# Gated recurrence and a squared-ReLU MLP on one core: a block's last w_out products behind the next block's first w_in products, and keys and queries one piece earlier

## The chip, the cores and the metric

One core of one Trainium2 chip. The metric is the device time of one execution in microseconds (us), compared as the median of several runs of each kernel on the same chip. The kernel before takes 506.82 us (median of 3 runs, 506.09 to 507.06).

## The reference

Two stages, the second on the first one's output:

```python
f = 1.0 / (1.0 + np.exp(-f_logit))              # batch 4, 8 heads, 768 steps, width 48
for t in range(S):
    state = f[:, :, t, :, None] * state + np.einsum('bhd,bhe->bhde', k[:, :, t], v[:, :, t])
    y[:, :, t] = np.einsum('bhd,bhde->bhe', q[:, :, t], state)
x = y.transpose(0, 2, 1, 3).reshape(3072, 384)
h = x @ w_in                                    # 384 x 2048
g = np.maximum(h, 0.0) ** 2
out = g @ w_out                                 # 2048 x 384
```

## The kernel before

**Blocks and units.** The 768 steps are six blocks of 128; with the batch of 4, a block is 512 columns of x. A block's recurrence is computed in four units (pairs of heads; the fourth is put together from leftover rows of the other three). `Unit` has stages that are named by letters: L and v load, G is the sigmoid of the gates (ScalarE, L426), K the keys (a scan and a product on VectorE, L431 and L437, with two clamps on GpSimd, L436), Q the queries (reciprocal, scan, product: L443, L445, L448), T and N transpose the keys (TensorE L481, ScalarE copies), D and S are products on TensorE (L505, L516), M and C mask and carry the state on VectorE (L523, L538, L543), Y the outputs on TensorE (L564, L576), H and X split the result into the two float32r parts of x (ScalarE L593, VectorE L598). After a fourth unit, `parts` (L605) moves the leftover rows from the tile `ys` into x by six small DMAs.

**The MLP.** `Moe` walks over 16 slices f of the hidden width. A piece n is `up(f)`: nine matmuls of 128x512 with w_in into a PSUM bank `ph` (L247), then ScalarE's ReLU, square and cast to `gh` (L257 to L259) and VectorE's `rest`, the remainder `gl` (L264), which frees the bank; and, two pieces later (LAG = 2), `down(f)`: nine matmuls with w_out into the three banks `po` (L273). There are two banks `ph` in turn, so `up(f)` waits until `rest(f-2)` is done; only the last block has a third bank. `run` writes this order out:

```python
for n in range(len(self.fs) + LAG):
    if n < len(self.fs):
        ...            # up, square, rest of slice n, with hooks between
    if n >= LAG:
        self.down(self.fs[n - LAG])
    for hook in hooks.get((n, 1), ()):
        hook()
```

So a block ends with two `down` in a row, and the next one begins with three `up` in a row, since it has no `down` of its own before its third piece. Between them `finish` (L317) copies the three `po` to SBUF (`ob`, ScalarE and VectorE) and issues three DMAs to the output on SyncE's queue (L326); for the second half of block 0 it adds them on VectorE to `part`, what `keep` saved of the first half (L310), and sends `part` out (L322, L326).

**Order of the work.** All four engines' orders are as written: the table FIRST and SECOND for block 0's and block 1's units and the first eight slices of block 0, then the list `order`: block 1, the second half of block 0 (slices 8 to 15), blocks 2, 3, 4, 5. This document calls the six places between them B1 (first half of block 0 to block 1), B2 (block 1 to second half of block 0), B3 (to block 2), B4 (2 to 3), B5 (3 to 4) and B6 (4 to 5). `up`, `down`, `rest` with a prime, as `up(0')`, are the block's that begins there. The 16 later units (blocks 2 to 5) are hooked to pieces, counted through all blocks: SLOTS gives each unit's piece `at` (D, S, M, C there, Y of the unit before it), and STAGE_AT puts the other stages some pieces ahead, at a place in the piece (0 before `up`, 0.5 before `rest`, 0.7 behind it, 1 behind `down`). Unit slot 18 is the third piece after B2.

**Shared buffers.** `ob`, `gh` and `gl` share tags of three buffers each. `part` shares one buffer with `junk`, into which ScalarE writes while `sizes` (L157) sums the weights, one product per piece in blocks 2 and 3; the first of these hooks is at piece 0 of block 2, so it waits until `part` has gone out.

Of the kernel before, what the change touches and what calls it, by code (L numbers as in the profile page):

```python
# [12 lines left out]
F32 = mybir.dt.float32  # L13
# [7 lines left out]
ALU = mybir.AluOpType  # L21
ET = mybir.EngineType

P = 128
# [7 lines left out]
NT = B * TB  # L32
# [3 lines left out]
NJ = DM // P  # L36
# [9 lines left out]
LAG = 2  # L46
# [10 lines left out]

STAGE_AT = ((-5, 0, "Lv"), (-2, 1, "GK"), (-1, 0.5, "Q"), (-1, 1, "TN"))  # L60
LAST_AT = ((-5, 0, "v"),)

SLOTS = (12, 14, 18, 20, 22, 28, 31, 34, 37, 44, 47, 50, 53, 60, 63, 66, 69)
# [11 lines left out]
c3 E0 W0 A4 i5 o2 R1 A7 O1 h3 d1 U2 C4 s4 o3 I4 B2 J3 M4 Y4 E1 U3 i6 Q5 c4 P1 W1 R2 E2 H4 X4 L6 G6 K6 o4  # L75
R3 J4 O2 v5 B3 S5 A5 U4 I5 M5 c5 d2 O3 E3 d3 D5 P2 C5 I7 r5 T6 J5 N6 P3 s5 A6 B4 I6 c6 o6 W2 O4 Q6 Y5 H5
X5 o5 U5 B5 W3 B7 B6 c7 R4 J6 m5 O6 R5 J7 E4 D6 S6 v7 C6 m6 r6 s6 U7 M6 O5 d5 Y6 d6 E5 d4 H6 X6 U6 P5 O7
P4 D7 S7 C7 r7 M7 R6 E6 P6 W4 s7 Y7 H7 X7 R7 h7 E7 W5 g7 d7 P7 W6 W7
"""


class Moe:
# [182 lines left out]
            out=gl, in0=self.ph.pop(f), in1=gh.bitcast(F32), op=ALU.subtract  # L265
        )

    def down(self, f, es=range(NJ)):
        gh, gl = self.g[f]
        for e in es:  # L270
            wh, wl = (self.w[f, 1][:, i, e * P : (e + 1) * P] for i in range(2))
            for i, (l, r) in enumerate(((wh, gl), (wl, gh), (wh, gh))):
                self.nc.tensor.matmul(  # L273
                    self.po[e], lhsT=l, rhs=r, start=f == self.fs[0] and i == 0,
                    stop=f == self.fs[-1] and i == 2,
                )

    def run(self, hooks, obs=None):

        for n in range(len(self.fs) + LAG):  # L280
            self.at = n
            if obs and n == len(self.fs):
                for e in range(NJ):
                    for f in self.fs[-LAG:]:
                        self.down(f, (e,))
                    for _, cs in tails(e):
                        self.nc.vector.tensor_copy(out=obs[e][:, cs], in_=self.po[e][:, cs])
                return
            if n < len(self.fs):
                for hook in hooks.get((n, 0), ()):  # L290
                    hook()
                f = self.fs[n]
                self.up(f)
                self.square(f)
                for hook in hooks.get((n, 0.5), ()):
                    hook()
                self.rest(f)
                for hook in hooks.get((n, 0.7), ()):
                    hook()
            if n >= LAG:  # L300
                self.down(self.fs[n - LAG])
            for hook in hooks.get((n, 1), ()):
                hook()
# [3 lines left out]
        t = self.gp.tile([P, NJ, NZ * CZ], F32, tag="part", name=name, bufs=1)  # L307
        return [t[:, e, :NT] for e in range(NJ)]

    def keep(self):  # L310

        part = self.third_of(f"part{self.blk}")
        for e in range(NJ):
            (self.nc.vector.tensor_copy if e % 2 else self.nc.scalar.copy)(out=part[e], in_=self.po[e])
        return part

    def finish(self, dst, part=None):  # L317
        nc = self.nc
        for e in range(NJ):
            if part:  # L320
                ob = part[e]
                nc.vector.tensor_tensor(out=ob, in0=self.po[e], in1=ob, op=ALU.add)  # L322
            else:
                ob = self.gp.tile([P, NT], F32, tag=("gh", "gl")[e % 2], name=f"ob{self.blk}_{e}")
                (nc.vector.tensor_copy if e % 2 else nc.scalar.copy)(out=ob, in_=self.po[e])
            nc.sync.dma_start(dst(e), ob)  # L326


def tails(e):

    if e < NJ - 1:
        return ((1, slice(0, NT)),)
    return ((0, slice(0, NT // 2)), (1, slice(NT // 2, NT)))
# [10 lines left out]
def fast_path(ctx, tc, moe, ident, low, fkqT, vN, w, w4, out):  # L344
    nc = tc.nc
# [20 lines left out]
    for r in (0, C):  # L366
        G.affine_select(
            out=mask[r : r + C], in_=mask[r : r + C], compare_op=ALU.is_ge, fill=0.0,
# [12 lines left out]
    def weights_load(f, i, mark=False):  # L381
        raw = moe.words(f, i)
        if mark:

            V.memset(raw[0:1, 0:1], 0)
        nc.sync.dma_start(raw, w[f, i].bitcast(I16)[:, 1:])
# [254 lines left out]
    xs = {blk: moe.new_x(blk, blk) for blk in range(2)}  # L641
# [66 lines left out]
    with tc.manual_schedule(engines={ET.PE, ET.SP, ET.DVE, ET.Activation}):  # L708
        with tc.tile_pool(name="ps_p", bufs=2, space=bass.MemoryType.PSUM) as ps_p:
            for t in FIRST.split():  # L710
                step(t)
        moe.psum(ctx, "ps_h1", "ps_o")

        moe.sums_of()
        for t in SECOND.split():
            step(t)
        part = moe.keep()
        whole = half[0] + half[1]
        order = [(1, whole), (0, half[1])] + [(blk, whole) for blk in range(2, NBLK)]
        hooks = [{} for _ in order]  # L720

        def hook(k, n, at, do):
            while n >= len(order[k][1]):
                k, n = k + 1, n - len(order[k][1])
            hooks[k].setdefault((max(n, 0), at), []).append(do)

        def third():
            early.close()
            moe.inputs(ctx)
            xs[2] = moe.new_x(2, 2)  # L730

        halves = [(f, i) for f in half[1] for i in range(2)]
        steps = {}

        def advance(h):
            if h not in steps:
                steps[h] = moe.decode(moe.row[halves[h]], lambda: moe.parts(*halves[h]))
            next(steps[h], None)  # L740

        for n in range(1, NF - 1):
            few = range(3 * (n - 1) // 2, min(3 * n // 2, len(halves)))
            for h in few:
                if n < AHEAD:
                    weights_load(*halves[h])
                else:
                    hook(0, n - AHEAD, 0.5, lambda h=h: weights_load(*halves[h], mark=True))

            def before(few=few):  # L750
                for h, last in zip(few, (None, *few)):
                    for m in (h, h, last):
                        if m is not None:
                            advance(m)

            def after(few=few[:-1]):
                for h in few:
                    advance(h)

            def last(few=few):  # L760
                for h in few[-1:]:
                    advance(h)
                    advance(h)


            for place, do in zip((0, 0.5, 0.7) if n > 1 else (0.7, 0.7, 0.7), (before, after, last)):
                hook(0, n, place, do)
        hook(0, 12, 0, third)
        later = [Unit(n, xs, (ps_a,)) for n in range(2 * HP, NBLK * HP)]
        for un, last, at in zip((*later, None), (None, *later), SLOTS):  # L770
            if un:
                for n, place, stage in STAGE_AT if un.own else LAST_AT:
                    hook(0, at + n, place, lambda un=un, stage=stage: un.stage(stage))

            def slot(un=un, last=last):
                for who, stage in (last, "Y"), (un, "DS"), (last, "HX"), (un, "rMC"), (un, "m" * bool(un and un.own)):
                    if who:
                        who.stage(stage)
                if last and not last.own:
                    last.stage("hg")  # L780

            hook(0, at, 0.7, slot)
            if un:
                hook(0, at + 1, 0, lambda un=un: un.stage("s"))

        for n in range(2 * NF):
            hook(2 + n // NF, n % NF, 1, lambda n=n: moe.sizes(n // 2, n % 2))
        general = []
        found = verdict(nc, moe, low, ident, ps_a)
        for n in range(2):  # L790
            hook(len(order) - 2, VERDICT_AT + n, 1, lambda: general.append(next(found)))
        hook(
            len(order) - 1, VERDICT_AT, 1,
            lambda: general.append(nc.values_load(general[1][0:1, 0:1], min_val=0, max_val=1)),
        )
        for k, (blk, fs) in enumerate(order):
            if blk > 1 and blk + 1 < NBLK:
                xs[blk + 1] = moe.new_x(blk + 1, (0, 1, 2)[blk - 2])
            moe.start(blk, xs[blk], fs)
            if blk == NBLK - 1:  # L800

                moe.third_bank = ps_a
                obs = moe.third_of("ob_last")
                moe.run(hooks[k], obs)
                moe.third_bank = None
            else:
                moe.run(hooks[k])
                moe.finish(lambda e: out[blk, e * P : (e + 1) * P], None if blk else part)
    return general[2], obs


# [203 lines left out]
```

## Time and profile before

| | |
|---|---|
| median of 3 runs | 506.82 us (506.09 to 507.06) |
| profiled execution | 504.94 us, of which span 503.2 us |
| PE (matmul) busy | 481.3 us, 96% of the span |
| ACT busy | 294.1 us, 58% |
| DVE busy | 237.8 us, 47% |
| POOL busy | 28.4 us, 6% |
| mean granted TensorE clock | 0.996 |

PE is TensorE's matmul, PEld its weight load, DVE VectorE, ACT ScalarE, POOL GpSimd, SP SyncE, whose queue (SPq) issues most DMAs. "idle before <-releaser" is the time an engine stood still before an instruction and what ended it. The chain of waits follows the work that ended last back to the start. Matmuls overlap in the records, so a nine of 128x512 products is read from where one nine starts to where the next does.

### The profile page before, as it was taken

The numbers are of one execution on the slowest core, as the hardware profiler recorded it, in microseconds if no ns is written. First come the engines' busy times: TensorE is split into PE (matmuls) and PEld (weight loads), VectorE is DVE, ScalarE is ACT, GpSimd is POOL, SyncE is SP. The second block draws the span as 40 slices with busy tenths as digits, with TensorE's granted clock in tenths as the row PEclk, the third lists the DMA queues.
The fourth block names the chain that finished last, engine by engine and source line by source line (L and its number), as shares of the span: only waits on it lengthen the run. The fifth ranks groups of instructions, "written<-read, shape, count | busy, mean of one in ns | idle before, by whom it ended". The sixth has DMA issues, their size and how long they took to land.

```text
span 503.2 us, 11462 instructions
## 1 busy us (share of the span) xinstructions
PE 481.3 (96%) x4831; PEld 383.7 (76%) x4831; DVE 237.8 (47%) x444; ACT 294.1 (58%) x615; POOL 28.4 (6%) x66
## 2 busy tenths in 40 slices
PE   3979999999998999999999999999999999999995
PEld 2667777888786887788888788888788877888884
DVE  7979963556734472563361444352346232211112
ACT  5569875877545553766664767564565544544441
POOL 6131010000000000000000000000000000000000
PEclk9999999999998999999999999999999999999999
DMA  8978007560214017203014313004410002100001
GB/s 263 310 259 278 13 7 245 187 228 27 89 29 151 3 18 196 62 17 90 3 26 136 102 28 92 1 7 117 141 29 12 1 1 33 64 1 1 0 1 68
DMA packets 20588, 41.96 MB, mean 83 GB/s; under 512 B 2752, under 2 KB 6192, under 8 KB 20528
## 3 DMA queue, kind: packets, MB, share of 16 engines
q1 hardware_dynamic: 19936, 40.09, 25.8%
q0 software_dynamic: 448, 0.92, 0.9%
q8 instruction: 40, 0.66, 0.6%
q14 instruction: 20, 0.16, 0.1%
q10 hardware_dynamic: 144, 0.13, 0.1%
HBM read 31.68 MB, written 4.72 MB: 72 GB/s over the span
## 4 chain that ended last, share of the span: by engine, by line
PE 90%; DVE 3%; ACT 3%; DMA 1%; issue 1%; SPq 0%; POOL 0%; ACTq 0%
PE po L273 41%; PE ph L247 38%; PE ds L516 2%; PE ds L505 2%; PE py L564 2%; PE pk L481 2%; PE ph L564 1%; PE ph L576 1%; DVE fkq L431 1%; PE py L576 1%; DMA vn<-in_vN_dram 1%; PE ph L667 1%; ACT gh L259 1%; ACT ph L257 1%; ACT ph L258 1%
## 5 line engine op out<-in xcount | busy, mean ns | idle before, releaser
L247 PE MATMUL ph<-x,w 128*128 128x512 f32 x864 | 219.8, 400 | 4.8 <-DVE sc L523 2.7
L247 PEld LDWEIGHTS ph<-x,w 128*128 128x128 f32 x864 | 161.6, 189 | 44.6 <-POOL low L436 3.0
L273 PE MATMUL po<-gh,w 128*128 128x512 f32 x576 | 180.9, 395 | 0.0
L264 DVE TENSOR_TENSOR gl<-ph,gh 128x512 fp32r<-128x512 f32 x96 | 66.3, 690 | 225.1 <-ACT gh L259 225.0
L257 ACT ACTIVATE ph<-ph 128x512 f32<-128x512 f32 x96 | 56.0, 583 | 129.5 <-PE ph L247 129.5
L273 PEld LDWEIGHTS po<-gh,w 128*128 128x128 f32 x576 | 108.3, 188 | 25.1
L273 PE MATMUL po<-gl,w 128*128 128x512 f32 x288 | 115.9, 403 | 0.6 <-DVE gl L264 0.6
L273 PEld LDWEIGHTS po<-gl,w 128*128 128x128 f32 x288 | 54.1, 188 | 14.5 <-DVE gl L264 1.3
L259 ACT CAST gh<-ph 128x512 fp32r<-128x512 f32 x96 | 56.3, 587 | 3.0
L258 ACT ACTIVATE ph<-ph 128x512 f32<-128x512 f32 x96 | 55.9, 582 | 3.0
L436 POOL TENSOR_SCALAR fkq<-fkq 128x8 f32<-128x8 f32 x18 | 11.0, 609 | 307.0 <-DVE fkq L431 263.9
L475 ACT COPY sx<-sp 48x208 f32<-48x208 f32 x44 | 16.0, 365 | 15.5 <-DVE sp L538 15.2
L431 DVE TENSOR_TENSOR_SCAN fkq<-fz,dr 128x520 f32<-128x520 f32 x18 | 22.2, 1232 | 1.1 <-ACT fz L426 1.1
L445 DVE TENSOR_TENSOR_SCAN fkq<-fz,dz 128x520 f32<-128x520 f32 x18 | 22.4, 1242 | 0.6
L131 ACT CAST head<-raw 128x384 f16<-128x384 bf16 (+1 forms) x33 | 19.3, 627 | 4.9 <-DMA raw<-in_w_dram 4.8
L564 PEld LDWEIGHTS py<-sc,vn 64*48 64x48 f32 (+1 forms) x384 | 16.2, 126 | 7.3 <-issue 7.3
L564 PE MATMUL py<-sc,vn 64*48 64x64 f32 (+1 forms) x384 | 20.6, 222 | 0.0
L576 PE MATMUL py<-rx,sx 48*48 48x64 f32 x192 | 19.3, 215 | 0.0
L143 ACT CAST w<-wa 128x384 fp32r<-128x384 f32 (+1 forms) x33 | 16.5, 510 | 3.6 <-DVE wa L134 3.2
L145 DVE TENSOR_TENSOR w<-wa,w 128x384 fp32r<-128x384 f32 (+1 forms) x33 | 17.9, 548 | 1.1 <-ACT w L143 0.6
L481 PE MATMUL pk<-ident,fkq 128*128 128x128 f32 x72 | 12.0, 293 | 6.3 <-POOL x L700 3.9
L134 DVE SCALAR_TENSOR_TENSOR wa<-raw,head 128x384 int32<-128x384 int32 (+1 forms) x33 | 17.6, 548 | 0.7 <-ACT head L131 0.6
(104 smaller groups left out, 462.6 us busy)
## 6 DMA issues: line engine op xcount, KB each, us to landing
raw<-in_w_dram SPq DMA_DIRECT2D x32, 383.8 KB, 5.8
fkq<-in_fkqT_dram SPq DMA_DIRECT2D x15, 768.0 KB, 5.0
vn<-in_vN_dram SPq DMA_DIRECT2D x24, 192.0 KB, 4.8
out_dram<-ob SPq DMA_DIRECT2D x12, 256.0 KB, 2.1
fkq<-in_fkqT_dram SPq DMA_DIRECT2D x9, 256.0 KB, 6.1
x<-ys SPq DMA_DIRECT2D x30, 64.0 KB, 2.4
last_kq<-fkq SPq DMA_DIRECT2D x28, 64.5 KB, 2.3
out_dram<-part SPq DMA_DIRECT2D x3, 256.0 KB, 2.1
```

What stands on the lines that cost most here:

```text
L131: nc.scalar.copy(out=self.upper(head, F16), in_=high)
L247: self.nc.tensor.matmul(self.ph[f], lhsT=w[:, i], rhs=x[:, j], start=first and n == 0, stop=last and n == 2)
L257: nc.scalar.activation(ph, ph, AF.Relu)
L258: nc.scalar.activation(ph, ph, AF.Square)
L259: nc.scalar.copy(out=gh, in_=ph)
L264: self.nc.vector.tensor_tensor(out=gl, in0=self.ph.pop(f), in1=gh.bitcast(F32), op=ALU.subtract)
L273: self.nc.tensor.matmul(self.po[e], lhsT=l, rhs=r, start=f == self.fs[0] and i == 0, stop=f == self.fs[-1] and i == 2,)
L431: V.tensor_tensor_scan(out=rr[:, ::-1], data0=self.fz[:, NZ * CZ : 0 : -1], data1=dr[:, ::-1], initial=0.0, op0=ALU.mult, op1=ALU.add,)
L445: V.tensor_tensor_scan(out=pp, data0=self.fz[:, : NZ * CZ], data1=dz, initial=0.0, op0=ALU.mult, op1=ALU.add)
L481: nc.tensor.transpose(out=self.pk[:, b], in_=self.kt[:, b * TB : (b + 1) * TB], identity=ident)
L564: nc.tensor.matmul(self.py[c][h * C : h * C + m, b * C : (b + 1) * C], lhsT=self.vn[rows, b, h * D : h * D + m], rhs=self.sc[rows, h, b], ...
L576: nc.tensor.matmul(self.py[c][h * C : h * C + m, b * C : (b + 1) * C], lhsT=s[rows, b * D : b * D + m], rhs=q[rows], start=False, stop=b = ...
```

## The change

It has two parts. First, `down` of a block's last slice no longer stands at the end of that block: `run` stops before it, and the next block's `run` calls it (with the evacuation of `po` behind it) after its own first `up`, square and `rest`. The last block still ends as before. Second, STAGE_AT puts G and K of the later units at the end of piece at-3 (it was at-2) and Q into piece at-2 (it was at-1); loads, T and everything from the slot on stay.

```diff
-STAGE_AT = ((-5, 0, "Lv"), (-2, 1, "GK"), (-1, 0.5, "Q"), (-1, 1, "TN"))
+STAGE_AT = ((-5, 0, "Lv"), (-3, 1, "GK"), (-2, 0.5, "Q"), (-1, 1, "TN"))
...
-P4 D7 S7 C7 r7 M7 R6 E6 P6 W4 s7 Y7 H7 X7 R7 h7 E7 W5 g7 d7 P7 W6 W7
+P4 D7 S7 C7 r7 M7 R6 E6 P6 W4 s7 Y7 H7 X7 R7 h7 E7 W5 g7 d7 P7 W6
...
-    def down(self, f, es=range(NJ)):
-        gh, gl = self.g[f]
+    def down(self, f, es=range(NJ), of=None):
+        po, g, fs = of or (self.po, self.g, self.fs)
+        gh, gl = g[f]
...
-    def run(self, hooks, obs=None):
+    def run(self, hooks, obs=None, before=None):
+
 
         for n in range(len(self.fs) + LAG):
+            if before and not obs and n == len(self.fs) + LAG - 1:
+                return
...
+            if before and n == 0:
+                before()
+                self.sums_of()
             if n >= LAG:
                 self.down(self.fs[n - LAG])
...
+    def ending(self, end):
+
+        of, f = (self.po, self.g, self.fs), self.fs[-1]
+
+        def do():
+            self.down(f, of=of)
+            end(of[0])
+
+        return do
...
-        part = moe.keep()
+        part = []
+        owed = moe.ending(lambda po: part.extend(moe.keep(po)))
...
-            moe.start(blk, xs[blk], fs)
+            moe.begin(blk, xs[blk], fs)
...
-                moe.run(hooks[k], obs)
+                moe.run(hooks[k], obs, owed)
...
-                moe.run(hooks[k])
-                moe.finish(lambda e: out[blk, e * P : (e + 1) * P], None if blk else part)
+                moe.run(hooks[k], None, owed)
+                owed = moe.ending(
+                    lambda po, blk=blk: moe.finish(
+                        lambda e: out[blk, e * P : (e + 1) * P], None if blk else part, po, blk
+                    )
+                )
```

**PE at B3.** `po_8_*` is the second half of block 0, `ph_0`, `ph_1` and `ph_2` are block 2's first slices. PE before, at the end of the second half of block 0:

```order
L273 MATMUL po_8_0_1987<-gl_15_2452,w_1_1682 128x512
L273 MATMUL po_8_0_1987<-gh_15_2451,w_1_1682 128x512 x2
L273 MATMUL po_8_1_1988<-gl_15_2452,w_1_1682 128x512
L273 MATMUL po_8_1_1988<-gh_15_2451,w_1_1682 128x512 x2
L273 MATMUL po_8_2_1989<-gl_15_2452,w_1_1682 128x512
L273 MATMUL po_8_2_1989<-gh_15_2451,w_1_1682 128x512 x2
L247 MATMUL ph_0_2496<-x_0_1706,w_0_375 128x512 x3
L247 MATMUL ph_0_2496<-x_1_1707,w_0_375 128x512 x3
L247 MATMUL ph_0_2496<-x_2_1708,w_0_375 128x512 x3
L247 MATMUL ph_1_2514<-x_0_1706,w_0_360 128x512 x3
```

PE now, at the same place:

```order
L247 MATMUL ph_0_2478<-x_0_1711,w_0_375 128x512 x3
L247 MATMUL ph_0_2478<-x_1_1712,w_0_375 128x512 x3
L247 MATMUL ph_0_2478<-x_2_1713,w_0_375 128x512 x3
L274 MATMUL po_8_0_2011<-gl_15_2452,w_1_1682 128x512
L274 MATMUL po_8_0_2011<-gh_15_2451,w_1_1682 128x512 x2
L274 MATMUL po_8_1_2012<-gl_15_2452,w_1_1682 128x512
L274 MATMUL po_8_1_2012<-gh_15_2451,w_1_1682 128x512 x2
L274 MATMUL po_8_2_2013<-gl_15_2452,w_1_1682 128x512
L274 MATMUL po_8_2_2013<-gh_15_2451,w_1_1682 128x512 x2
L247 MATMUL ph_1_2514<-x_0_1711,w_0_360 128x512 x3
```

The old block's last nine stands between the new block's first and second nine; behind it `up(1')`, `up(2')` and `down(0')` follow as before. B1, B2, B4, B5 and B6 change in the same way.

**DVE at B2.** `gl_15` is block 1's last remainder, `gl_8` and `gl_9` the first two of block 0's second half; the `fkq_2` rows (a scan, shown as SCALAR_TENSOR_TENSOR, a product, a reciprocal, a scan, a product) are K and Q of the unit at slot 18. DVE before, at block 1's end:

```order
L264 TENSOR_TENSOR gl_15_1946<-ph_15_1842,gh_15_1945 128x512
L325 COPY ob_1_1981<-po_0_1_1262 128x512
L264 TENSOR_TENSOR gl_8_2001<-ph_8_1990,gh_8_2000 128x512
L431 SCALAR_TENSOR_TENSOR fkq_2_1785<-fz_71,dr 128x520
L437 TENSOR_TENSOR fkq_2_1785<-fkq_2_1785 128x512
L443 RECIPROCAL dz<-fkq_2_1785 128x8
```

DVE now, at the same place:

```order
L264 TENSOR_TENSOR gl_15_1946<-ph_15_1842,gh_15_1945 128x512
L448 SCALAR_TENSOR_TENSOR fkq_2_1788<-fz_71,dr 128x520
L454 TENSOR_TENSOR fkq_2_1788<-fkq_2_1788 128x512
L460 RECIPROCAL dz<-fkq_2_1788 128x8
L462 SCALAR_TENSOR_TENSOR fkq_2_1788<-fz_71,dz 128x520
L465 TENSOR_TENSOR fkq_2_1788<-fkq_2_1788 128x512
L264 TENSOR_TENSOR gl_8_1985<-ph_8_1974,gh_8_1984 128x512
L342 COPY ob_1_2005<-po_0_1_1284 128x512
L264 TENSOR_TENSOR gl_9_2029<-ph_9_2018,gh_9_2028 128x512
```

Keys and queries moved ahead of the new block's first remainder, and the copy of `po` behind it.

**DVE and ACT at B3.** `gl_0` to `gl_2` are block 2's first remainders. DVE before, at the end of the second half of block 0:

```order
L264 TENSOR_TENSOR gl_15_2452<-ph_15_2339,gh_15_2451 128x512
L322 TENSOR_TENSOR part_1249<-po_8_0_1987,part_1249 128x512
L322 TENSOR_TENSOR part_1249<-po_8_1_1988,part_1249 128x512
L322 TENSOR_TENSOR part_1249<-po_8_2_1989,part_1249 128x512
L264 TENSOR_TENSOR gl_0_2507<-ph_0_2496,gh_0_2506 128x512
L264 TENSOR_TENSOR gl_1_2525<-ph_1_2514,gh_1_2524 128x512
L264 TENSOR_TENSOR gl_2_2546<-ph_2_2535,gh_2_2545 128x512
L431 SCALAR_TENSOR_TENSOR fkq_1_2438<-fz_71,dr 128x520
```

DVE now, at B3:

```order
L264 TENSOR_TENSOR gl_0_2489<-ph_0_2478,gh_0_2488 128x512
L339 TENSOR_TENSOR part_1279<-po_8_0_2011,part_1279 128x512
L339 TENSOR_TENSOR part_1279<-po_8_1_2012,part_1279 128x512
L339 TENSOR_TENSOR part_1279<-po_8_2_2013,part_1279 128x512
L264 TENSOR_TENSOR gl_1_2525<-ph_1_2514,gh_1_2524 128x512
L448 SCALAR_TENSOR_TENSOR fkq_1_2438<-fz_71,dr 128x520
```

ACT now, at B3, with the semaphores that each instruction waits for (DMAHW is a DMA's; the three here are those of the DMAs that send `part` out):

```order
L259 CAST gh_0_2488<-ph_0_2478 128x512 [waits Activation_49]
L157 ACTIVATE junk,sums<-w_0_375 128x384 [waits DMAHW4_49,DMAHW5_49,DMAHW3_49,DVE_49]
L257 ACTIVATE ph_1_2514<-ph_1_2514 128x512 [waits PE_49]
L258 ACTIVATE ph_1_2514<-ph_1_2514 128x512 [waits Activation_49]
L259 CAST gh_1_2524<-ph_1_2514 128x512 [waits Activation_49]
```

The three additions to `part` moved behind `gl_0`, and K (with Q behind it) ahead of `gl_2`. On ACT these five rows stand in the same order, with the same waits, as before.

## Rows read from the trace of the kernel before

**Rows 1.** The page, part 1: busy us (share of the span) xinstructions of TensorE.

```profile
PE 481.3 (96%) x4831; PEld 383.7 (76%) x4831; DVE 237.8 (47%) x444; ACT 294.1 (58%) x615; POOL 28.4 (6%) x66
```

**Rows 2.** Waits of PE, longest first: us in total, times, longest us.

```profile
PE pk L481 <- DVE fkq L437: 2.4, 1, 2.4
PE ph L247 <- DVE gl L264: 1.6, 3, 0.5
PE ph L247 <- DVE raw L385: 0.5, 1, 0.5
```

**Rows 3.** The chain of waits at B4 and B6: start us, us, what.

```profile
275.23 2.12 PE ph L247 x9
279.96 2.38 PE ph L247 x9
282.34 2.10 PE po L273 x9
...
430.64 6.32 PE ph L247 x27
```

**Rows 4.** The chain: a piece with T undisturbed, and B2's first and third nine.

```profile
123.90 2.10 PE po L273 x9
126.43 2.11 PE ph L247 x9
...
151.38 2.12 PE ph L247 x9
...
159.12 3.01 PE ph L247 x9
```

**Rows 5.** Stretches at B2: busy us (xinstructions) of each engine, PEclk, DMA share, GB/s.

```profile
155.60:158.00 2.40, 0.00 (x1) 0.00 (x1) 2.31 (x3) 1.93 (x4) 0.64 (x1) 0.91 0.67 250
158.00:161.00 3.00, 3.00 (x9) 2.57 (x10) 2.74 (x4) 0.70 (x2) 0.27 (x2) 0.50 0.00 0
```

**Rows 6.** DVE's timeline, keys and queries in block 2: start us, us, instruction [idle before].

```profile
221.20 0.69 DVE L264 TENSOR_TENSOR gl<-ph,gh 128x512 fp32r<-128x512 f32 x1 [3.04 <-ACT gh L259]
221.81 1.23 DVE L431 TENSOR_TENSOR_SCAN fkq<-fz,dr 128x520 f32<-128x520 f32 x1
...
226.02 0.68 DVE L264 TENSOR_TENSOR gl<-ph,gh 128x512 fp32r<-128x512 f32 x1
```

**Rows 7.** B1: the chain at block 0's last nines, x's last DMAs, and their landing.

```profile
72.48 6.50 PE po L273 x27
...
73.94 1.78 SPq L605 DMA_DIRECT2D x<-ys  x3
...
DMA to landing us min/median/max: 2.5/3.0/3.5
```

**Rows 8.** Timelines of DVE, SP and ACT at B3, put in order of time.

```profile
187.16 4.14 SPq L605 DMA_DIRECT2D x<-ys  x6
...
195.58 2.09 DVE L322 TENSOR_TENSOR part<-po,part 128x512 f32<-128x512 f32 x3 [2.36 <-PE po L273]
196.30 1.73 SPq L326 DMA_DIRECT2D out_dram<-part  x3
199.09 0.58 ACT L257 ACTIVATE ph<-ph 128x512 f32<-128x512 f32 x1 [6.59 <-PE ph L247]
200.80 0.53 ACT L157 ACTIVATE junk<-w 128x384 f32<-128x384 f32 x1
200.94 0.69 DVE L264 TENSOR_TENSOR gl<-ph,gh 128x512 fp32r<-128x512 f32 x1 [3.26 <-ACT gh L259]
201.31 0.59 ACT L257 ACTIVATE ph<-ph 128x512 f32<-128x512 f32 x1
203.17 0.69 DVE L264 TENSOR_TENSOR gl<-ph,gh 128x512 fp32r<-128x512 f32 x1 [1.54 <-ACT gh L259]
```

**Rows 9.** The page, part 6: DMA issues, KB each, median us from issue to landing.

```profile
out_dram<-ob SPq DMA_DIRECT2D x12, 256.0 KB, 2.1
fkq<-in_fkqT_dram SPq DMA_DIRECT2D x9, 256.0 KB, 6.1
```

More of the change, by code (lines that the diff above doesn't have):

```diff
@@ L273, in down @@
                 self.nc.tensor.matmul(
-                    self.po[e], lhsT=l, rhs=r, start=f == self.fs[0] and i == 0,
-                    stop=f == self.fs[-1] and i == 2,
+                    po[e], lhsT=l, rhs=r, start=f == fs[0] and i == 0, stop=f == fs[-1] and i == 2,
                 )
-    def run(self, hooks, obs=None):
+    def run(self, hooks, obs=None, before=None):
         for n in range(len(self.fs) + LAG):
+            if before and not obs and n == len(self.fs) + LAG - 1:
+                return
             self.at = n
@@ L308, in third_of, with keep, finish @@
         return [t[:, e, :NT] for e in range(NJ)]
-    def keep(self):
-        part = self.third_of(f"part{self.blk}")
+    def keep(self, po):
+        part = self.third_of("part0")
         for e in range(NJ):
-            (self.nc.vector.tensor_copy if e % 2 else self.nc.scalar.copy)(out=part[e], in_=self.po[e])
+            (self.nc.vector.tensor_copy if e % 2 else self.nc.scalar.copy)(out=part[e], in_=po[e])
         return part
-    def finish(self, dst, part=None):
-        nc = self.nc
+    def ending(self, end):
[4 more added lines that the diff above has]
+        return do
+    def finish(self, dst, part=None, po=None, blk=None):
+        nc, po = self.nc, po or self.po
+        blk = self.blk if blk is None else blk
         for e in range(NJ):
@@ L321, in finish @@
                 ob = part[e]
-                nc.vector.tensor_tensor(out=ob, in0=self.po[e], in1=ob, op=ALU.add)
+                nc.vector.tensor_tensor(out=ob, in0=po[e], in1=ob, op=ALU.add)
             else:
-                ob = self.gp.tile([P, NT], F32, tag=("gh", "gl")[e % 2], name=f"ob{self.blk}_{e}")
-                (nc.vector.tensor_copy if e % 2 else nc.scalar.copy)(out=ob, in_=self.po[e])
+                ob = self.gp.tile([P, NT], F32, tag=("gh", "gl")[e % 2], name=f"ob{blk}_{e}")
+                (nc.vector.tensor_copy if e % 2 else nc.scalar.copy)(out=ob, in_=po[e])
             nc.sync.dma_start(dst(e), ob)
```

## The prediction

> **What bounds the kernel now.** TensorE. I read the busy times first: PE is busy 96% of the span [rows 1], so only what it waits for, or what slows it, can be gained. The list of PE's waits comes next. After the first 60 us it has five entries that matter: 2.4 us once, for a product of K at a transpose, and four waits of 0.5 us of a w_in nine, three put down to `gl` and one to a small memset behind it [rows 2]. The chain of waits shows where they are: the four lie at B1, B3, B4 and B5, in front of `up(2')`, the long one at B2.
>
> **What a boundary costs.** At B4 three nines take from 275.23 to 282.34, 7.11 us. At B6, where the last block has a third bank, 27 products take 6.32 us [rows 3]. So a nine is 2.1 us, and one such boundary costs 0.8 us: the wait and the restart. The cause is in the rows at B3: `rest(0')` begins 1.85 us after `up(0')` is handed to ScalarE (199.09 to 200.94) and takes 0.69 us, 2.5 us in all, while only `up(1')`, 2.1 us, covers it [rows 8].
>
> At B2 the cost is larger. From the first nine's start (151.38) to the third one's end (159.12 + 3.01 = 162.13) it takes 10.75 us [rows 4]. Undisturbed, three nines and a transpose group T (126.43 less 126.00, 0.43 us) take 6.32 + 0.43 = 6.75 us [rows 3, 4]. So B2 loses 4.0 us: 2.4 us of waiting [rows 2], and 1.6 us because the granted clock stands at 0.50, 1.2 instead of 2.4 GHz, in the 3 us behind it [rows 5].
>
> **The change, part by part.** Nothing is added or removed; the same instructions run in another order, and no DMA passes another one on SP or POOL.
>
> *B4 and B5.* `up(2')` now has `down(15)` and `up(1')` ahead of it, 4.2 us of cover against 2.5 us. Saved: 0.8 us each. What could be late next is `cast(1')`, since its buffer `gh` is the one that `ob` 0 leaves when its DMA has landed. Counting from the end of `up(0')`: ScalarE ends `cast(0')` at 1.85 and the copy of `po` 0 at 2.45, landing takes 2.1 us [rows 9], so 4.6; `cast(1')` is due at about 5.4. It holds. K and Q of the unit four pieces on now stand between `rest(1')` and `rest(2')`: they take 4.2 us (221.81 to 226.02) [rows 6], so `rest(2')` ends near 4.2 + 2.5 + 4.2 + 0.7 = 11.6, and `up(4')` is due at 6 x 2.1 = 12.6. It holds, by 1.0 us.
>
> *B6.* No wait before, none after: 0.
>
> *B2.* K and Q now stand behind `gl_15`, with `down(13)`, `down(14)` and `up(0')` to hide them, 6.3 us of PE against 4.2 us; `rest(0')` comes behind them in time, and the transposes find their keys done. The wait goes, and with it the stretch at half clock: 4.0 us. A new small wait: Y of that slot writes into the bank that `rest(1')` frees at 4.2 + 2.5 = 6.7, and PE comes there at 2.1 + 2.1 + 0.43 + 2.1 less the start's lead of 0.2, 6.5. I take 3.7 us.
>
> *B1.* `up(0')` moves 2.1 us earlier, to 72.48 + 4.2 = 76.7. It reads x, whose last rows come by DMAs: SP issues three within 73.94 to 75.72, and they land 2.5 to 3.5 us after their issue [rows 7]. The third, issued about 75.1, lands between 77.6 and 78.6; its products are due at 76.7 + 1.4 = 78.1. The first, issued at 73.94, lands between 76.4 and 77.4, due at 76.7. Today the old block's last nine hides this. I take 0.6 us of new wait (none to 0.9) against 0.8 saved: 0.2 us gained. B3's x stays hidden: its six DMAs are issued by 187.16 + 4.14 = 191.3, so they have landed by 194.8, about where `down(15)`, whose place `up(0')` takes, begins today (its first third ends where `part` is first added, 195.58) [rows 8]. At B4 to B6 a block's fourth unit is written three pieces ahead of the end instead of two, 4.2 us more.
>
> *B3.* Here the cover goes. `part` is added and sent out behind `rest(0')`, and ScalarE's first product into `junk`, which shares the buffer, waits for the landing, with `relu(1')` behind it in ScalarE's order. Today `part` has left long ago: its DMAs are issued from 196.30 on, `junk` runs at 200.80 [rows 8]. After, from the start of `relu(0')`: `rest(0')` ends at 1.85 + 0.69 = 2.54, three additions take 2.09, the third DMA is issued at 4.6 and lands 2.1 later [rows 9], 6.7 to 6.9. Then `junk` 0.51, `relu(1')` at 7.3, `rest(1')` from 9.1 to 9.8 (1.86 + 0.69 behind `relu(1')`) [rows 8]. `up(3')` needs it after `down(15)`, `up(1')`, `up(2')`, `down(0')`, at 4 x 2.1 less 0.2 = 8.2: a wait of 1.6 us. Behind `rest(1')` stand K and Q, 4.2 us, so `rest(2')` ends near 14.7, and `up(4')` is due at 9.9 + 4.2 = 14.1: 0.5 us more, and 0.2 us for two restarts. B3 costs 2.3 us where it cost 0.8: 1.5 us lost.
>
> *K and Q elsewhere.* Nothing waits for keys at the other slots, so nothing is gained. At five slots they now follow the slot's own VectorE work; there VectorE stands idle 3.04 us ahead of the next remainder [rows 6], so this comes 4.2 - 3.0 = 1.2 us later, and it is due only 6.3 us after its `up`, while it ends 2.5 after it. Cost 0.
>
> Sum: 0.8 + 0.8 + 3.7 + 0.2 - 1.5 = 4.0 us. The profiled execution, 504.94 us (span 503.2), would become 500.9. The median of the runs is 506.82, 1.88 us above it, so I forecast **502.8 us**.
>
> **A rule against it.** Four waits of 0.53 us each leave the granted clock where it was (it drops only at B2, and the page's mean is 0.996); the one of 2.4 us brings 0.50 [rows 2, 5]. The Trainium skill, page "TensorE: Matmul & The Clock Gate", section "A second HAM failure mode: psum-queue depth-cycling", says that frequent small idle stretches of TensorE between groups of products, from cycling PSUM banks, make the clock swing between its two levels. By that rule B3's new pair of waits could bring 1.2 GHz back, which is rival 1; the four short waits here do not bear it out.
>
> **Rivals.**
> 1. *The clock falls at B3.* The new wait there is 1.6 us, between the 0.53 that left the clock alone and the 2.4 that did not. The price is B2's, 1.6 us: 504.4 us. For it: a second wait follows two nines later. Against: it is shorter than B2's.
> 2. *`junk` does not hold ScalarE up* (the additions or the landing are sooner than I count). Then B3 gains 0.8 instead of losing 1.5: 500.5 us. Against it: the wait stands in the order, and it would have to end 1.6 us sooner.
> 3. *The output's landing becomes the bound.* At B2, B4 and B5 `cast(1')` waits for `ob` 0. It decides from a landing of about 3.9 us on (2.45 + 3.9 = 6.35; 0.95 later than due, which uses up the 1.0 us of `up(4')`). With the 6.1 us that loads of the same size take [rows 9], `cast(1')` is 3.1 us late; B4 and B5 then lose 1.5 us as B3 does, instead of gaining 0.8, and B2 keeps 0.6. Sum 0.2 + 0.6 - 1.5 - 1.5 - 1.5 = -3.7: 510.5 us. Against it: the twelve landings have a median of 2.1 us, and at these places the same load is queued only behind them.
> 4. *Half of it is eaten* by waits of VectorE or ScalarE that I hold to be hidden (decoding steps of block 1 behind the earlier K, Q): about 506, within what can be told.
>
> **How the numbers follow.** Forecast 0.55; rival 1 0.18; rival 2 0.11; rival 4 0.10; rival 3 0.06. A measurement of this kernel tells about 0.2%, 1.0 us, from no change. Forecast and rivals 1 and 2 are faster by more: 0.84; rival 4 makes up 0.10 within it; rival 3 is the 0.06 slower. The range goes from rival 2 to rival 1, with half of the three runs' spread (0.97 us) at either end: 500.0 to 504.9. It leaves out rivals 3 and 4, 0.16.
>
> **What would show it.** Right: in PE's waits the one for K's product is gone, and the 0.5 us ones at B4 and B5; granted clock 1.00 throughout B2; a new wait of `up(3')` at B3 of about 1.6 us, put down to `gl`, with ScalarE idle ahead of `junk` until a DMA of `part` lands, and a second one of about 0.5; short waits for `x<-ys` at B1. Wrong: PE waiting for `gl` at B4 or B5 with ScalarE's `cast` held by `out_dram<-ob` (rival 3), a stretch at 0.50 behind B3 (rival 1), or no wait there (rival 2).

## The result, and the profile after

The changed kernel takes 502.56 us (median of 11 runs, 500.42 to 505.66) against 507.58 us (11 runs, 505.94 to 509.01) for the kernel before on the same chip: ratio 0.9902, 95% interval 0.9878 to 0.9926. The profiled execution of the changed kernel takes 502.94 us, its span is 501.2 us at a mean granted clock of 0.992.

The page, part 1, of the changed kernel answers to [rows 1]; TensorE is as much the bound as it was.

```profile
PE 480.2 (96%) x4827; PEld 384.1 (77%) x4831; DVE 237.2 (47%) x444; ACT 292.6 (58%) x615; POOL 28.4 (6%) x66
```

PE's waits in the changed kernel, which answer to [rows 2] (lines below the first function have moved: K's product is L454, T is L498):

```profile
PE pk L498 <- DVE fkq L454: 3.8, 1, 3.8
...
PE ph L247 <- DVE gl L264: 1.6, 1, 1.6
```

The 3.8 us are the first T of the prologue, before 7 us; the trace of before has them too, as 3.9 us put down to a memset of x. Behind the prologue the wait for K's product and the four waits of 0.5 us (three for `gl`, one put down to a memset of `raw`) are gone; one of 1.6 us has come at B3, and one of 0.2 us at B1.

The chain of waits of the changed kernel at B1 (80.03), B2 (154.31 to 158.94), B3 (193.59 to 210.62) and B4 (277.31 on), with the same columns as [rows 3]:

```profile
75.45 4.40 PE po L274 x18
80.03 2.67 PE ph L247 x9
...
154.31 2.09 PE po L274 x9
156.41 2.10 PE ph L247 x9
158.94 2.10 PE ph L247 x9
...
193.59 2.12 PE ph L247 x9
197.58 0.69 DVE gl L264
198.27 1.80 DVE part L339 x3
200.09 2.41 DMA out_dram<-part
202.60 0.62 ACT junk L157 x2
204.96 0.70 DVE gl L264
205.71 2.37 PE ph L247 x9
208.08 2.10 PE po L274 x9
210.62 2.26 PE ph L247 x9
...
277.31 4.21 PE ph L247 x18
281.53 2.10 PE po L274 x9
```

At B2 and B4 the chain is TensorE alone, every nine 2.1 us, with 0.43 us for T in front of 158.94. At B3 it leaves TensorE: a remainder, the three additions to `part`, the landing of `part`, ScalarE's first product into `junk`, the second remainder, and only then the fourth w_in nine. The stretch that stood at half clock in [rows 5] has the full one (same columns):

```profile
158.00:161.00 3.00, 3.00 (x16) 2.15 (x14) 0.61 (x1) 2.35 (x5) 0.00 (x0) 1.00 0.88 285
```

**Place by place.** All executions have the same 870 w_in and 864 w_out products. Setting the start of the k-th of a kind in one trace against the k-th in the other shows where time came or went. The numbers are microseconds against the execution of before that is shown ahead of the prediction; minus is a gain:

| execution | up to B1 | B1 | B2 | B3 | B4 | B5 | B6 |
|---|---|---|---|---|---|---|---|
| forecast | 0 | -0.2 | -3.7 | +1.5 | -0.8 | -0.8 | 0 |
| changed | +2.96 | -0.04 | -3.84 | +1.25 | -0.81 | -0.80 | 0 |
| e1 stage only | +3.07 | -0.01 | -3.65 | 0 | 0 | 0 | 0 |
| e2 down only | +1.65 | -0.17 | -2.33 | +1.27 | -0.81 | -0.80 | 0 |
| e3 junk later | +3.33 | +0.04 | -3.85 | -0.80 | -0.81 | -0.80 | 0 |
| e4 B3 as before | +3.23 | -0.09 | -3.85 | 0 | -0.81 | -0.80 | 0 |
| e5 third first | +1.19 | -0.80 | -3.85 | -0.80 | -0.81 | -0.80 | 0 |
| e6 changed again | +4.07 | -0.16 | -3.85 | +1.24 | -0.81 | -0.80 | 0 |
| e7 junk later again | +4.07 | -0.11 | -3.85 | -0.80 | -0.81 | -0.80 | 0 |
| e8 before again | +3.65 | -0.01 | +0.18 | 0 | 0 | 0 | 0 |

Between B2 and B3 every other execution is another 0.27 to 0.34 us ahead of the one shown of before (e8 below). Behind the last w_out product the spans end between 0.55 us earlier and 0.31 us later than that of before; e3 and e7, which are one and the same kernel, lie 0.86 us apart there, so this is spread too. The places of the changed kernel sum to -4.24 us; its span is only 2.0 us shorter because its prologue took 2.96 us longer, with 0.34 us less between B2 and B3 and 0.38 us less behind the last product. The 2.96 us are the prologue's own spread, for which see e8; a median over runs averages over it, two single profiles do not.

### The profile page after: what moved, and what is told of

Same layout as the page of the kernel before. It is cut to its first block, busy times and chain, and to the rows that moved or that the text cites. A ratio compares the mean times of both kernels' runs of the same rounds, so it can differ in the third digit from the quotient of the medians.

```text
span 501.2 us, 11466 instructions
## 1 busy us (share of the span) xinstructions
PE 480.2 (96%) x4827; PEld 384.1 (77%) x4831; DVE 237.2 (47%) x444; ACT 292.6 (58%) x615; POOL 28.4 (6%) x66
## 4 chain that ended last, share of the span: by engine, by line
PE 91%; DMA 3%; DVE 2%; ACT 1%; issue 1%; SPq 0%; ACTq 0%
PE po L274 40%; PE ph L247 40%; PE ds L533 2%; PE ds L522 2%; PE py L581 2%; DMA raw<-in_w_dram 2%; PE pk L498 1%; DMA vn<-in_vN_dram 1%; PE ph L581 1%; PE ph L593 1%; PE py L593 1%; DMA out_dram<-part 0%; PE first_py L581 0%; DVE gl L264 0%; DVE part L339 0%
## 5 line engine op out<-in xcount | busy, mean ns | idle before, releaser
L157 ACT ACTIVATE junk<-w 128x384 f32<-128x384 f32 x32 | 16.8, 527 | 5.1 <-DMA out_dram<-part 5.1
```

## Experiments

### e1 and e2: each half of the change alone

e1 is the kernel before with one line of the change:

```diff
-STAGE_AT = ((-5, 0, "Lv"), (-2, 1, "GK"), (-1, 0.5, "Q"), (-1, 1, "TN"))
+STAGE_AT = ((-5, 0, "Lv"), (-3, 1, "GK"), (-2, 0.5, "Q"), (-1, 1, "TN"))
```

> The kernel before with the new STAGE_AT alone. My theory: keys and queries (4.2 us of VectorE) stand ahead of the new block's first remainder at B2, so the 2.4 us wait for K's product and the half clock behind it go, and what is left there is the wait for gl that other places have, shortened by the transposes (0.43 us) to about 0.1 us with its restart: B2 gains about 3.6 us. B1, B3, B4 and B5 keep their 0.5 us waits. In all 3.6 us faster than before. Rival, that the gain at B2 comes from the moved products: B2 gains under 1 us here.

Measured: 504.07 us (12 runs) against 506.96 (23 runs), ratio 0.9926 (0.9899 to 0.9953). By place B2 gains 3.65 us and nothing else moves. The chain of e1 at B2:

```profile
154.45 2.12 PE ph L247 x9
157.82 0.60 ACT gh L259
158.44 0.70 DVE gl L264
159.19 2.36 PE ph L247 x9
```

K's wait has gone and the short wait for `gl` stands there, as at the other boundaries; T, at 158.50 to 159.10, fills all but 0.1 us of it. The rival, that the moved products make the gain at B2, falls: B2 gained nearly all of it with the products where they were.

e2 is the changed kernel with the other line:

```diff
-STAGE_AT = ((-5, 0, "Lv"), (-3, 1, "GK"), (-2, 0.5, "Q"), (-1, 1, "TN"))
+STAGE_AT = ((-5, 0, "Lv"), (-2, 1, "GK"), (-1, 0.5, "Q"), (-1, 1, "TN"))
```

> The changed kernel with the old STAGE_AT. My theory: at B2 VectorE does the first remainder (ends 2.5 us behind the first nine), a copy of po (0.7), then K's scan and product (1.9): K is done about 5.1 us behind the first nine, and the transposes are due at 4.2. So 0.9 us of the 2.4 us wait stay. If a wait of that length leaves the granted clock at 1.00, B2 gains about 2.7 us; if it falls to 0.50 again, about 1.2 us. B3 loses 1.2 us as in the changed kernel, B4 and B5 gain 0.8 each, B1 nothing. In all 3.1 us faster than before, 1.2 slower than the changed kernel. Rival, that the moved products alone cover K: no wait for K at B2, 4.3 us faster than before.

Measured: 503.51 us (12 runs) against 506.96, ratio 0.9941 (0.9918 to 0.9965). B2 gains 2.33 us, not 2.7. PE's wait for K is back at half its length; the row is from e2's list of PE's waits, the next ones from its chain, and the last two from its stretches (columns of [rows 5]):

```profile
PE pk L498 <- DVE fkq L454: 1.2, 1, 1.2
```

```profile
150.76 2.12 PE ph L247 x9
154.61 1.08 ACT ob L342 x2
156.26 1.25 DVE fkq L448
...
158.28 0.66 PE pk L498 x4
```

```profile
155.00:158.00 3.00, 2.07 (x9) 1.32 (x7) 2.75 (x4) 2.09 (x5) 0.36 (x1) 1.00 0.60 233
158.00:161.00 3.00, 2.72 (x14) 2.04 (x14) 2.80 (x5) 1.59 (x4) 0.56 (x2) 1.00 0.93 279
```

The wait is 1.2 us instead of 0.9 since K's scan waits for the gates: on ScalarE they stand behind the two copies of `po` (L342), which I had not counted. The granted clock stays at 1.00 through it. So cutting the wait by 1.2 us gained 2.33: the other 1.1 us are of the 1.6 us that the prediction put down to the half clock. The remaining 0.5 us of those need not be the clock's: of the 4.0 us that B2 lost, e2 still loses 1.7 at full clock, 1.2 of it waiting; the restart behind the wait is in the rest (T takes 0.66 us there instead of 0.44). The two halves overlap: alone they gain 3.65 and 2.84 us by place (2.33 + 0.17 + 0.81 + 0.80 - 1.27), together 4.24. What the moved products add to the earlier keys is 0.6 us, because B3 gives back most of B4 and B5. The medians put the two halves in the other order, 2.9 us for e1 and 3.5 for e2; their intervals, 2.4 to 5.1 and 1.8 to 4.2 us, overlap too far to rank them, and hold the sums by place.

### e3 and e4: what holds B3

e3 is the changed kernel with the products into `junk` two pieces later:

```diff
-            hook(2 + n // NF, n % NF, 1, lambda n=n: moe.sizes(n // 2, n % 2))
+            hook(2, n + 2, 1, lambda n=n: moe.sizes(n // 2, n % 2))
```

> The changed kernel with the 32 summing products of ScalarE hooked two pieces later, so that none of them stands between the first and the second piece of block 2. My theory: ScalarE no longer waits there for the DMAs of part, the 1.6 us wait of the fourth w_in nine at B3 goes, and B3 gains 0.8 us against before instead of losing 1.2: 2.0 us faster than the changed kernel, 6.3 faster than before. Rival, that B3's wait comes from VectorE (three additions of 1.9 us in all ahead of the second remainder, keys and queries behind it): the wait stays, with ScalarE's second cast early and the time that of the changed kernel.

Measured: 500.71 us (6 runs) against 506.96, ratio 0.988 (0.9852 to 0.9908). The wait is gone and B3 gains 0.80 us where the changed kernel loses 1.25: 2.05 us. The chain of e3 at B3 is TensorE alone:

```profile
196.14 2.09 PE po L274 x9
198.24 4.21 PE ph L247 x18
202.45 2.10 PE po L274 x9
```

The three additions and the earlier keys and queries stand in VectorE's order as in the changed kernel, so the rival that VectorE holds B3 falls. It is ScalarE's wait for a buffer, for a sum that nothing needs so soon.

e4 closes the second half of block 0 in the old order, and only it:

```diff
...
-            if before and not obs and n == len(self.fs) + LAG - 1:
+            if not (close or obs) and n == len(self.fs) + LAG - 1:
                 return
...
-                moe.run(hooks[k], None, owed)
+                moe.run(hooks[k], None, owed, blk == 0)
+                if blk == 0:
+                    moe.finish(lambda e: out[blk, e * P : (e + 1) * P], part)
+                    owed = None
+                    continue
```

> The changed kernel with the old order at B3 alone: the last nine of block 0's second half, the additions and their DMAs stand ahead of block 2 again. My theory: the idle time of ScalarE ahead of its first summing product and the 1.6 us wait go, the old wait of 0.5 us for gl comes back, B3 is as before, the rest as in the changed kernel: 1.2 us faster than the changed kernel, 5.5 faster than before. Rival, that the loss at B3 comes from the earlier keys and queries and not from the moved nine: it stays, and the time is that of the changed kernel.

Measured: 501.63 us (6 runs) against 506.96, ratio 0.9891 (0.9864 to 0.9918). B3 costs what it did before, to 0.01 us; its chain shows the old short wait:

```profile
199.94 0.70 DVE gl L264
200.68 2.37 PE ph L247 x9
```

So the loss at B3 comes from the moved nine, not from the earlier keys.

### e5 to e7: what holds B1, and the best version

e5 is e3 with a third of the moved nine left ahead of the new block at B1:

```diff
+        moe.down(half[0][-1], (0,))
         part = []
-        owed = moe.ending(lambda po: part.extend(moe.keep(po)))
+        owed = moe.ending(lambda po: part.extend(moe.keep(po)), (1, 2))
...
-    def ending(self, end):
+    def ending(self, end, es=range(NJ)):
...
-            self.down(f, of=of)
+            self.down(f, es, of=of)
```

> The kernel with the later summing products, and at B1 the first third (three products) of the old block's last nine ahead of the new block's first w_in nine, two thirds behind it. My theory: B1 gains nothing in the changed kernel because the first nine comes 2.1 us earlier and then waits for the DMAs of x's last rows: 0.2 us ahead of its start and again between its thirds. Three products, 0.7 us, in front of it cover that; the other six (1.4 us) still cover the remainder that the third w_in nine needs (2.1 + 1.4 = 3.5 us against 2.5). B1 then gains 0.8 us less a rest of 0.1: 0.7 faster than with the later summing products alone, 2.7 faster than the changed kernel. Rival, that B1 is held by something that does not depend on when the first nine starts (the remainder, or the copies that save po): no gain over the later summing products alone.

e6 and e7 are the changed kernel and e3 again, on the chip of e5.

> The changed kernel once more, beside the other two on one chip. By the places measured so far it is 4.3 us faster than before in everything behind the prologue; what the prologue takes differs from one execution to the next by up to 3 us with the granted clock there, so the median may stand 4 to 5 us below that of before.

> The kernel with the later summing products once more: 2.0 us faster than the changed kernel on the same chip.

Measured against 507.71 us of before (11 runs): e5 500.49 us, ratio 0.9853 (0.9825 to 0.9882); e6 503.21, 0.9908 (0.9885 to 0.9931); e7 500.20, 0.9842 (0.9814 to 0.987); 6 runs each. The chain at B1, of e3 and then of e5:

```profile
80.34 1.76 PE ph L247 x6
82.21 0.95 PE ph L247 x3
```

```profile
78.78 2.10 PE ph L247 x9
80.88 1.39 PE po L274 x6
82.27 4.22 PE ph L247 x18
```

In e3 the first nine stops before its last third; in e5 it runs through in 2.10 us, and B1 gains 0.80 us. What held B1 depends on when the nine starts, as the landing of x does and the remainder does not. The waits of TensorE's weight loads (PEld) name it. This row is from the changed kernel; the five other executions that begin block 1 with the same nine have it with 0.4 to 0.8 us, and e5, e1 and both executions of the kernel before have no wait for `x<-ys` at all:

```profile
PEld ph L247 <- DMA x<-ys: 0.7, 2, 0.4
```

By place e5 stands 0.7 us ahead of e7, as expected. The medians do not show these 0.7 us: e5 and e7 lie 0.29 us apart the wrong way round, and each ranges over 3 to 4.5 us (498.13 to 501.44, 498.11 to 502.61). Both are faster than the changed kernel: e7's interval lies wholly below e6's, e5's just so too (0.9882 against 0.9885). Between the medians e7 is 3.0 us faster than e6, not the 2.0 expected; by place it is 1.99. Where the other 1.0 us comes from the runs do not show; e7's range over 4.5 us.

### e8: the kernel before once more

> The kernel before once more, for a second profiled execution. Two questions. The products S ahead of B3 took 0.33 us longer in the execution shown of before than in every execution of the other kernels: if that belongs to the kernel before, it is here too; if it belongs to that one execution, S is short here. And the prologue: every other execution has stretches at half clock ahead of 37 us, the one shown of before has none; if that is chance, this one has them too, starts block 0's first nines up to 4 us later, and its time is 506 to 509 us.

Measured: 508.07 us. The products S ahead of B3 are 0.28 us shorter here than in the first execution of the same kernel (30 of them, L516, take 0.72 us, not 0.99), so those 0.3 us belong to that one execution and not to the change. At B2 e8 loses 0.18 us more than the first execution did, so the gain there is known to about 0.2 us. And the prologue takes 3.65 us longer. Two stretches of it, of the first execution of before and of e8 (columns of [rows 5]):

```profile
22.00:26.00 4.00, 2.96 (x164) 2.77 (x157) 3.55 (x9) 1.94 (x5) 0.00 (x0) 1.00 0.99 328
26.00:32.00 6.00, 3.31 (x42) 2.56 (x36) 5.86 (x10) 3.89 (x8) 1.12 (x2) 1.00 1.03 393
```

```profile
22.00:26.00 4.00, 1.61 (x85) 1.45 (x76) 2.54 (x6) 1.51 (x3) 0.00 (x0) 0.93 1.00 346
26.00:32.00 6.00, 3.47 (x82) 3.29 (x84) 4.47 (x9) 2.90 (x7) 0.97 (x2) 0.50 1.00 378
```

The first execution of before is the one whose clock never fell here; the same program's did fall in e8, to 1.2 GHz throughout 26 to 32 us. So one and the same kernel differs by 3.65 us up to B1, and the 2.96 us of the changed kernel need no cause in the change. By place the changed kernel stands 5.2 us ahead of e8, of which 0.7 us is prologue, against 5.0 between the medians.

## Why the prediction was right

The forecast was 502.8 us and the median is 502.56; by place 4.0 us were forecast and 4.24 came. Point by point:

**B4 and B5** were sized right, 0.81 and 0.80 against 0.8. Rival 3 would have shown as ScalarE waiting for `out_dram<-ob` ahead of the second cast; ScalarE's timeline at B4 has none, the cast follows the square at once, as it does at B2 and B5:

```profile
280.07 0.58 ACT L258 ACTIVATE ph<-ph 128x512 f32<-128x512 f32 x1
280.68 0.59 ACT L259 CAST gh<-ph 128x512 fp32r<-128x512 f32 x1
```

Its condition was a landing of about 3.9 us for the first of the three stores, `ob` 0. That one took 2.15 us at B4, the two behind it 3.63 and 3.83, so the rival was nearer than the median of 2.4 us over all twelve makes it look.

**B2** was right: 3.84 against 3.7. The wait is gone, the granted clock is 1.00 throughout, and e1 and e2 show the keys' move to be the cause. The rest, 4.0 less 3.84, is 0.16 us. It fits the small wait of Y, taken at 0.25: Y takes 1.21 us here (161.04 to 162.25) and took 1.08 before. The share of the half clock in B2's loss was probably put too high: 1.6 us, where e2 got back 1.1 us beyond the wait that it cut. The sum did not suffer, because the whole loss went.

**B3** had the right mechanism and one term too many. ScalarE's and VectorE's timelines of the changed kernel, and T of PE's:

```profile
202.60 0.53 ACT L157 ACTIVATE junk<-w 128x384 f32<-128x384 f32 x1 [5.05 <-DMA out_dram<-part]
```

```profile
197.58 0.69 DVE L264 TENSOR_TENSOR gl<-ph,gh 128x512 fp32r<-128x512 f32 x1 [5.61 <-ACT gh L259]
...
204.96 0.69 DVE L264 TENSOR_TENSOR gl<-ph,gh 128x512 fp32r<-128x512 f32 x1 [4.90 <-ACT gh L259]
...
209.78 1.28 DVE L264 TENSOR_TENSOR gl<-ph,gh 128x512 fp32r<-128x512 f32 x2
```

```profile
205.71 2.37 PE L247 MATMUL ph<-x,w 128*128 128x512 f32 x9 [1.61 <-DVE gl L264]
...
210.03 0.60 PE L498 MATMUL pk<-ident,fkq 128*128 128x128 f32 x4
210.52 2.36 PE L247 MATMUL ph<-x,w 128*128 128x512 f32 x9
```

`junk` was forecast 6.7 to 6.9 us behind the start of `relu(0')` (195.73 in this trace), so at 202.4 to 202.6, and starts at 202.60; the wait of `up(3')` was forecast as 1.6 us and is 1.61. That it fits so closely is partly luck: the three additions took 1.87 us instead of 2.09, and the last landing of `part` 2.41 instead of 2.1, which nearly cancel. The step that failed is the second wait, 0.5 us ahead of `up(4')`: I counted K and Q on VectorE behind `rest(1')` but left out that T, 0.43 us of TensorE, stands ahead of `up(4')` there. `rest(2')`, the first of the two at 209.78, ends about 210.5, and the nine starts at 210.52, directly behind T: the remainder was in time by less than 0.1 us. The restart of the one wait that is left cost more than the 0.2 us counted for two: the nine takes 2.37 us instead of 2.10, and the gap around the wait is another 0.16. Loss 1.25 against 1.5.

Rival 1, that the clock falls at B3, did not come: 1.61 us of waiting left it at 1.00 here, and so did 1.2 us at B2 in e2; none of the waits for `gl` behind the prologue, of 0.5 to 1.7 us in all these runs, changed it. By the rule of the Trainium skill weighed in the prediction (page "TensorE: Matmul & The Clock Gate", section "A second HAM failure mode: psum-queue depth-cycling") B3 could have swung between the levels. No trace here agrees with that. Rival 2 fell with ScalarE's 5.05 us in front of `junk`.

**B1** was forecast at 0.2 us and gave 0.04; over the six executions with that order it goes from 0.04 lost to 0.17 gained. The wait for x's last rows was taken at 0.6 us: the first nine starts 0.18 us late (80.03 against 75.45 + 4.40) and takes 2.67 us instead of 2.10, 0.75 us in all, inside the bound of 0.9. e5 and the weight loads' waits for `x<-ys` show the cause.

**K and Q elsewhere**: 0, as forecast, and B6 too. Rival 4 finds no place where anything was eaten.

**From the sum to the median**: I carried 1.88 us from the profiled execution of before to the median of three runs. The direction was right, and e8 shows a reason: that execution had a prologue without a fall of the clock, and the other nine profiled ones each have a fall. That the forecast lies only 0.24 us from the median is partly luck. With 11 runs the median of before is 507.58, so the step is 2.64 us and not 1.88, and the medians differ by 5.0 us where 4.0 were forecast. The two errors nearly cancel. The 4.24 us by place are the better test of the sum; the interval of the medians' difference, 3.8 to 6.2 us, holds them.

## What to carry to other kernels

When a tail of one stage is moved behind the head of the next, follow everything that hung on the tail: each buffer that its evacuation frees and the first in-order instruction that wants that buffer (`junk` behind `part`, 1.25 us lost, and 2.05 gained by calling a sum that nobody waits for two pieces later), and each input of the head that the tail used to hide (x's rows at B1; three products of nine left in front were enough). A wait that brings the half clock costs more than its length: cutting B2's from 2.4 to 1.2 us returned 2.33. Its length alone does not tell whether it will: in the first execution of before TensorE stands idle for 2.69 us from 26.97 on, and the clock stays at 1.00 there, while the 2.40 us at B2 brought 0.50. And before two profiles are subtracted, line them up by the count of a repeated instruction and read the gain place by place; between the two single executions of before and after the prologue alone differed by 2.96 us.

## What the runs showed that I had not expected

The prologue. In nine of the ten profiled executions the granted clock falls to 1.2 GHz at some time before 37 us, at another moment and for another length in most of them, and the last w_out nines of block 0's first half start 1.2 to 4.1 us later than in the one execution where it does not. TensorE stands idle there for 2.0 to 3.0 us at a time in all of them, and in the execution without a fall it was busy 2.96 of the 4.00 us from 22 to 26, in e8 1.61. Why one execution escapes was not tried. It is as large as everything that the change gains, and no edit here touches it.
